# Places in on-chip memory: W_out tiles on one place modulo 256 bytes, token sums in steps of 128 bytes

## The chip, the cores and the metric

One core of a Trainium2 chip runs the program. The metric is device time in microseconds (us): the median of three runs, and beside it one profiled execution, whose trace is what the rows below are read from. TensorE multiplies matrices; for each product it loads a stationary operand (a weight load, PEld in the profile) and then streams a moving operand through it (PE). Both come from the on-chip memory, in which every tile has a place: an offset in bytes within each of the 128 partitions. Results go to the accumulation banks.

## The reference

The program computes block-causal attention for 8 batches of 8 heads, 576 positions and head size 64, and feeds it to a two-layer network.

```python
scores = scale * np.matmul(q, k.transpose(0, 1, 3, 2))
scores = np.where(mask, scores, -1000000000.0)        # blocks of 64
attn = np.exp(scores - max); attn = attn / (sum + 1e-09)
x = (attn @ v) as 4608 tokens of 512
h = x @ w_in                                          # 512 -> 2048
g = h * (1.0 / (1.0 + np.exp(-h)))
out = g @ w_out                                       # 2048 -> 512
```

All of it is in float32, and the weights arrive as 64-bit words.

## The kernel before

The tokens, W_in and W_out are each split into a high and a low part of a reduced float type, and a product is made of three matmuls: high by high, high by low, low by high. The order of the work on every engine is written out by hand, in a long list of steps (`a.load`, `ffn`, `i34.lo:3`, ...); the list is not part of the change, and every engine has the same instructions in the same order before and after it.

**First layer** (`ffn1`, L1063). W_in lies in `wi[0]` (high) and `wi[1]` (low), four rows `c` of 128 inputs each; it is the stationary operand, in pieces of 128 columns. The tokens lie in `xbuf` and are the moving operand, 448, 512 or 256 columns a matmul. Three matmuls follow each other on one row `c`, then three on the next. In the profile they are `h<-x,wi`: the moving tile is named first, the stationary one second. The attention's own matmuls (L719, L824) come between the calls of `ffn1` until about 556 us; the last calls of `ffn1` follow each other without them until about 623 us.

**Second layer** (`Item.prod`, L1140). It multiplies 2x2 blocks by Strassen's scheme in seven products. `Item` n (72 of them, four to a block of 256 tokens) forms seven sums of token quarters ("token sums"), high and low, in one of five slots, `slots()[n % 5]`; they are the stationary operand, 128 columns at a time. `Turned` d (0 to 7) holds the seven sums of W_out's quarters, high and low; it is the moving operand, 256 columns. An item has 42 matmuls: for each of the seven products two halves (d even, d odd), and for each of these the three matmuls high-high, high-low, low-high. Items n with n % 4 = 0 multiply by d = 0 and 1, then 2 and 3, 4 and 5, 6 and 7. In the profile these are `S<-ta,x`, `c<-tb,gc` and so on (S and c are accumulation banks).

Each tile's place modulo 256 bytes, as the program is built before the change:

| tile | role | place modulo 256 |
|---|---|---|
| `wi`, rows c = 0, 1, 2, 3 (8320 bytes each) | W_in, stationary in layer 1 | 128, 0, 128, 0 |
| `x` | tokens, moving in layer 1 | 192 |
| `ta` (d = 0, 1, 2) | W_out, moving in layer 2 | 128 |
| `tb` (d = 3, 4, 5) | W_out, moving | 0 |
| columns of `wi` (d = 6, 7) | W_out, moving | 128 for the first four products, 0 for the last three |
| `gc` (slot 0) | token sums, stationary | 64 for all |
| `x` (slots 1 and 4) | token sums | 192 for all |
| columns of `wi` (slots 2 and 3), 64 bytes on | token sums | 192 and 64 by row, high and low alike |

In slots 2 and 3 the place goes 192, 64, 192, 64, 192 in the course of an item's 42 matmuls, changing after 6, 12, 24 and 36 of them. The function that gives a tile its seven groups is `at`, and `of_wi` and `of_x` give them for columns of `wi` and for halves of `xbuf`.

Of the kernel before, what the change touches and what calls it, by code (L numbers as in the profile page):

```python
# [9 lines left out]
F32 = mybir.dt.float32  # L10
F32R = mybir.dt.float32r
# [8 lines left out]
DM, DFF = 512, 2048  # L20
P = 128
# [10 lines left out]
CT = DM // P  # L32
# [7 lines left out]
SHIFT = 16  # L40
# [357 lines left out]
def fills():  # L398

    out = [((0,), d, None) for d in range(LAG)]  # L400
    out += [((0, 1), d, f) for d in range(LAG, NSTEP) for f in range(2)]
    out += [((1,), d, None) for d in range(LAG)]
    out += [((2, 3), d, f) for d in range(NSTEP) for f in range(2)]
    out += [(("b", b), d, f) for b in range(B) for d in range(NSTEP) for f in range(2)]
    return out
# [39 lines left out]
def attn_ffn(ctx: ExitStack, tc: tile.TileContext, qk, v, qk0, v0, qk1, v1, w_in, w_out, out):  # L445
    nc = tc.nc
    pool = lambda name, bufs=1, **kw: ctx.enter_context(tc.tile_pool(name=name, bufs=bufs, **kw))
    cp = pool("const")
# [14 lines left out]
    pU = pool("pU", space=PSUM)  # L463
    pH = pool("pH", bufs=2, space=PSUM)

    wi = [cp.tile([P, CT, DFF + 2 * SHIFT], F32R, name=f"wi{t}") for t in range(2)]
    cp.tile([P, SHIFT], F32, name="gap0")
    xbuf = cp.tile([P, NX, 2, TB], F32R, name="x")
    cp.tile([P, SHIFT], F32, name="gap1")
    steps = fills()  # L470
    g_dram = {z[:2]: dp.tile([P, 2, width(z[0])], F32, name=f"gd{'_'.join(map(str, z[0]))}_{z[1]}") for z in steps}
    x_full, filled = {}, set()
# [106 lines left out]
    def groups(seven):  # L579

        return [seven[:, 0:2], seven[:, 2:3], seven[:, 3:5], seven[:, 5:7]]
# [2 lines left out]

        return g[0][:, j] if j < 2 else g[1][:, 0] if j == 2 else g[2][:, j - 3] if j < 5 else g[3][:, j - 5]

    def at(t, n):

        return [groups(t[:, 1792 * i + n : 1792 * i + n + 1792].rearrange("p (j m) -> p j m", j=7)) for i in range(2)]

    def of_wi(d, e, n):

        a, b = (slice(256 * k + n, 256 * k + n + 256) for k in (d, e))
        return [[w[:, 0:2, a], w[:, 2:3, a], w[:, 0:2, b], w[:, 2:4, b]] for w in wi]

    def of_x(t):

        def some(n, k):
            s = t[n : n + k]
            step = s[1] - s[0] if k > 1 else 1  # L600
            return slice(s[0], s[-1] + 1, step)

        return [[xbuf[:, some(n, k), i] for n, k in ((0, 2), (2, 1), (3, 2), (5, 2))] for i in range(2)]

    class Turned:

# [9 lines left out]
        def place(u):  # L616
            if u.d < NTA:
                t = pools["ta"].tile([P, 2 * 7 * 256 + (24 if u.d == NTA - 1 else 0)], F32R, tag=f"ta{u.d}", name="ta")
                u.g = at(t, 0)
            elif u.d < 6:  # L620
                t = sp.tile([P, 2, 7, 256], F32R, tag=f"tb{u.d}", name="tb")
                u.g = [groups(t[:, i]) for i in range(2)]
            else:
                u.g = of_wi(2 * u.d - 12, 2 * u.d - 11, 0)

# [450 lines left out]
    class Item:  # L1076
# [44 lines left out]
        def hi(u, k):  # L1121
            if k == 0:
                u.g = slots()[u.n % NSLOT]
            nc.scalar.copy(u.goal(0, k), u.source(k))  # L1124
# [21 lines left out]
    spare = []  # L1146

    def slots():
        if not spare:
            t = sp.tile([P, 2 * 7 * 256 + SHIFT], F32R, tag="gc", name="gc")  # L1150
            spare.extend([at(t, SHIFT), of_x(range(7)), of_wi(4, 5, SHIFT), of_wi(6, 7, SHIFT), of_x(range(8, 15))])
        return spare

    class Out:
# [53 lines left out]
    a, b = First(0), First(1)  # L1208
# [24 lines left out]
    for token in ORDER.split():  # L1233
        name, _, method = token.partition(".")
        if name.startswith("warm:"):
            warm(int(name[5:]))
        elif method:
            method, _, k = method.partition(":")
# [47 lines left out]
```

## Time and profile before

| | |
|---|---|
| median of three runs | 985.79 us (984.91 to 987.05) |
| the profiled execution | 985.77 us |
| its span, first to last instruction | 984.1 us |
| matmuls of layer 1 (L1063) | 1968 |
| matmuls of layer 2 (L1140) | 3024 |

Of the profiled execution, 1.7 us lie outside the span. Matmuls are pipelined: the profile gives each a duration of about 0.28 us for 256 columns, while the next one starts after 0.11 to 0.12 us. So a busy share does not tell how fast TensorE goes; the time from one start to the next does. From a row of the timeline that merges n matmuls, this step is (the row's us minus one duration) / (n - 1), or the difference of two rows' starts divided by the matmuls between them.

### The profile page before, as it was taken

The page shows a single profiled execution, that of the slowest core. Times are in us where ns is not written, and L with a number is a line of the kernel's source. Part 1 is how long each engine was busy: PE and PEld are TensorE (multiplying, and loading weights), DVE is VectorE, ACT ScalarE, POOL GpSimd, SP SyncE. Part 2 cuts the span into 40 slices and gives each one's busy share as a digit, 9 for nine tenths or more (in the row PEclk, how much of TensorE's full clock was granted, in tenths as well). Part 3 has the DMA queues.
Part 4 walks back from the last instruction along what each step waited for, and adds up shares of the span by engine and source line. Part 5 has one row for each costly group of instructions (what it writes and reads, how often), then busy time and mean ns, then how long its engine had stood idle before and what let it go on. Part 6 is the DMA issues. An engine that isn't in the chain of part 4 may idle for free.

```text
span 984.1 us, 20775 instructions
## 1 busy us (share of the span) xinstructions
PE 971.9 (99%) x6922; PEld 878.7 (89%) x6922; DVE 770.3 (78%) x1975; ACT 689.1 (70%) x1557; POOL 618.9 (63%) x724
## 2 busy tenths in 40 slices
PE   7999999999999999999999999999999999999998
PEld 7778778888888888888888899999999999999998
DVE  6868899899899999889999544598677777677661
ACT  5977777777777777777777455997667666767750
POOL 5666977988788787777887556654444443444430
PEclk9999999999999999999999999999999999999999
DMA  9966545554555545555554266655544544454511
GB/s 352 384 196 188 167 140 150 157 152 148 164 149 148 168 141 150 162 144 157 155 153 136 88 207 201 199 172 149 134 131 124 149 133 128 139 141 132 140 52 44
DMA packets 109803, 155.50 MB, mean 158 GB/s; under 512 B 18560, under 2 KB 83072, under 8 KB 109696
## 3 DMA queue, kind: packets, MB, share of 16 engines
q1 hardware_dynamic: 109696, 154.18, 52.4%
q8 instruction: 54, 0.88, 0.4%
q14 instruction: 53, 0.43, 0.1%
HBM read 106.95 MB, written 47.19 MB: 157 GB/s over the span
## 4 chain that ended last, share of the span: by engine, by line
PE 95%; DMA 2%; SPq 1%; DVE 1%; ACT 0%; POOL 0%; issue 0%; DVEq 0%; POOLq 0%
PE h L1063 42%; PE S L1140 24%; PE c L1140 10%; PE S L719 9%; PE U L824 9%; DMA wst<-in_moe_w_in_dram 1%; PE S L1004 1%; DMA raw<-gdb 1%; SPq L1088 1%; PE S L1035 0%; PE S L881 0%; DVE g L1175 0%; SPq L905 0%; POOL x L1128 0%; PE S L966 0%
## 5 line engine op out<-in xcount | busy, mean ns | idle before, releaser
L1063 PE MATMUL h<-x,wi 128*128 128x448 f32 (+2 forms) x1968 | 420.6, 369 | 1.7 <-POOL wi L576 0.9
L1063 PEld LDWEIGHTS h<-x,wi 128*128 128x128 f32 x1968 | 356.8, 188 | 38.3 <-POOL wi L576 1.1
L773 ACT ACTIVATE p<-T 128x512 f32<-128x512 f32 (+1 forms) x192 | 115.7, 614 | 29.3 <-DVE T L762 23.9
L658 DVE TRANSPOSE_TENSOR_REDUCE Mx<-S 64x4 f32<-64x128 f32 (+4 forms) x384 | 130.5, 399 | 6.1 <-PE S L719 5.1
L1069 ACT COPY g<-h 128x448 f32<-128x448 f32 (+1 forms) x160 | 86.1, 538 | 35.0 <-PE h L1063 25.4
L1128 POOL TENSOR_TENSOR x<-raw,x 128x512 fp32r<-128x512 f32 (+1 forms) x58 | 59.4, 1028 | 76.6 <-ACT x L1124 68.1
L779 POOL TENSOR_TENSOR pa<-p 128x448 f32<-128x448 f32 x64 | 73.6, 1151 | 49.7 <-ACT p L773 44.9
L1128 POOL TENSOR_TENSOR wi<-raw,wi 128x512 fp32r<-128x512 f32 (+1 forms) x56 | 57.2, 1025 | 72.2 <-ACT wi L1124 65.0
L700 POOL TENSOR_TENSOR qh<-qk,qh 64x576 fp32r<-64x576 f32 x64 | 91.7, 1433 | 5.3 <-DMA gd<-g 0.4
L719 PE MATMUL S<-qh 128*128 128x448 f32 (+3 forms) x320 | 92.1, 301 | 0.0
L824 PE MATMUL U<-p,v 128*64 128x448 f32 (+3 forms) x640 | 86.5, 416 | 0.0
L719 PE MATMUL S<-ql,qh 128*128 128x448 f32 (+3 forms) x320 | 83.9, 307 | 0.0
L694 ACT CAST qh<-qk 128x1024 fp32r<-128x1024 f32 x64 | 67.0, 1047 | 21.5 <-POOL pa L782 6.8
L704 POOL TENSOR_TENSOR ql<-qk,qh 128x448 fp32r<-128x448 f32 x64 | 73.6, 1151 | 10.6 <-issue 5.9
L824 PEld LDWEIGHTS U<-p,v 128*64 128x64 f32 x640 | 43.2, 136 | 40.8 <-issue 30.0
L1091 ACT ACTIVATE raw<-raw 128x1024 f32<-128x1024 f32 x72 | 76.5, 1063 | 0.0
L765 DVE TENSOR_TENSOR T<-S,MR 128x128 f32<-128x128 f32 (+2 forms) x192 | 73.5, 410 | 0.0
L719 PEld LDWEIGHTS S<-ql,qh 128*128 128x128 f32 (+1 forms) x320 | 57.1, 178 | 6.4
L719 PEld LDWEIGHTS S<-qh 128*128 128x128 f32 (+1 forms) x320 | 56.9, 178 | 3.1 <-issue 0.3
L782 POOL TENSOR_TENSOR pa<-pa,p 128x320 f32<-128x320 f32 x64 | 56.0, 875 | 3.7
L744 ACT COPY m<-m 32x14 f32<-32x14 f32 x192 | 38.8, 202 | 26.2 <-DVE m L740 24.7
L1128 POOL TENSOR_TENSOR gc<-raw,gc 128x512 fp32r<-128x512 f32 (+1 forms) x30 | 30.4, 1019 | 40.7 <-ACT gc L1124 33.2
(198 smaller groups left out, 2082.8 us busy)
## 6 DMA issues: line engine op xcount, KB each, us to landing
qk<-in_qk_dram SPq DMA_DIRECT2D x128, 256.0 KB, 3.9
gdb<-g SPq DMA_DIRECT2D x128, 224.0 KB, 2.6
raw<-gdb SPq DMA_DIRECT2D x64, 256.0 KB, 3.2
v<-in_v_dram SPq DMA_DIRECT2D x64, 160.0 KB, 2.3
wst<-in_moe_w_in_dram SPq DMA_DIRECT2D x16, 512.0 KB, 8.5
wst<-in_moe_w_out_dram SPq DMA_DIRECT2D x16, 512.0 KB, 4.8
gd<-g SPq DMA_DIRECT2D x32, 256.0 KB, 2.8
raw<-gd SPq DMA_DIRECT2D x32, 256.0 KB, 3.5
```

Source lines behind the costliest of these rows:

```text
L658: nc.vector.tensor_reduce(out=out, in_=in_, axis=AX.X, op=op, apply_transpose=True)
L700: nc.gpsimd.tensor_tensor(out=u.qh[r, c], in0=u.raw[r, c], in1=u.qh[r, c], op=ALU.subtract)
L704: nc.gpsimd.tensor_tensor(out=u.ql, in0=u.raw[:, :NQ], in1=u.qh[:, :NQ], op=ALU.subtract)
L719: nc.tensor.matmul(u.ps(c, w, m), u.kk[r, j * P : j * P + m], q[r, q0 : q0 + w], start=qq == 0 and not (ROWS and seg == 2), stop=qq == 1 a ...
L773: nc.scalar.activation(u.p[:, c:e], u.T[:, c:e], AF.Exp, scale=SCALE)
L779: nc.gpsimd.tensor_tensor(out=u.pa, in0=u.p[:, :NQ], in1=u.p[:, 960 : 960 + NQ], op=ALU.add)
L824: nc.tensor.matmul(U[64 * e : 64 * e + 64, q0 : q0 + w], y.vv[:, e, j], z.p[:, c : c + w], start=n == 0, stop=n == 4)
L1063: nc.tensor.matmul(o, wi[wt][:, c, w], x_of(g, c, xt), start=c + k == 0, stop=c == CT - 1 and k == 2)
L1069: nc.scalar.copy(g, hs.pop(z)[:, :n])
L1091: nc.scalar.activation(u.raw, u.raw, AF.Silu)
L1128: e.tensor_tensor(out=u.goal(1, k), in0=u.source(k), in1=u.goal(0, k), op=ALU.subtract)
L1140: nc.tensor.matmul(o, quarter(u.g[a], j)[:, P * e : P * e + P], quarter(turned[d].g[b], TORDER[FACTOR[pr]]), start=u.q == 0 and i % 2 == 0 ...
```

## The change

Rows of `wi` become 8448 bytes (33 times 256), the gap behind `x` grows from 64 to 192 bytes, `tb` gets the same layout as `ta`, and the token sums in `x` and `gc` are laid out with steps of 128 bytes between them.

```diff
-    wi = [cp.tile([P, CT, DFF + 2 * SHIFT], F32R, name=f"wi{t}") for t in range(2)]
+    wi = [cp.tile([P, CT, DFF + 4 * SHIFT], F32R, name=f"wi{t}") for t in range(2)]
     cp.tile([P, SHIFT], F32, name="gap0")
     xbuf = cp.tile([P, NX, 2, TB], F32R, name="x")
-    cp.tile([P, SHIFT], F32, name="gap1")
+    cp.tile([P, 3 * SHIFT], F32, name="gap1")
...
-    def at(t, n):
-
-        return [groups(t[:, 1792 * i + n : 1792 * i + n + 1792].rearrange("p (j m) -> p j m", j=7)) for i in range(2)]
-
-    def of_wi(d, e, n):
-
-        a, b = (slice(256 * k + n, 256 * k + n + 256) for k in (d, e))
+    def at(t, n, pitch=256, step=0):
+
+        out = [[], []]
+        for i, g in enumerate(out):
+            for j, w in ((0, 2), (2, 1), (3, 2), (5, 2)):
+                first = n + (7 * pitch + step) * i + pitch * j + step * (j > 2)
+                g.append(t[:, first : first + pitch * w].rearrange("p (j m) -> p j m", j=w)[..., :256])
+        return out
+
+    def of_wi(d, e, n, step=0):
+
+        a, b = (slice(256 * k + m, 256 * k + m + 256) for k, m in ((d, n), (e, n + step)))
         return [[w[:, 0:2, a], w[:, 2:3, a], w[:, 0:2, b], w[:, 2:4, b]] for w in wi]
 
-    def of_x(t):
-
-        def some(n, k):
-            s = t[n : n + k]
-            step = s[1] - s[0] if k > 1 else 1
-            return slice(s[0], s[-1] + 1, step)
-
-        return [[xbuf[:, some(n, k), i] for n, k in ((0, 2), (2, 1), (3, 2), (5, 2))] for i in range(2)]
+    def of_x(h):
+
+        return at(xbuf[:, 8 * h : 8 * h + 8].rearrange("p n i t -> p (n i t)"), 0, 256 + 2 * SHIFT)
...
-                t = sp.tile([P, 2, 7, 256], F32R, tag=f"tb{u.d}", name="tb")
-                u.g = [groups(t[:, i]) for i in range(2)]
+                t = sp.tile([P, 2 * 7 * 256], F32R, tag=f"tb{u.d}", name="tb")
+                u.g = at(t, 0)
...
-            t = sp.tile([P, 2 * 7 * 256 + SHIFT], F32R, tag="gc", name="gc")
-            spare.extend([at(t, SHIFT), of_x(range(7)), of_wi(4, 5, SHIFT), of_wi(6, 7, SHIFT), of_x(range(8, 15))])
+            t = sp.tile([P, 2 * 7 * 256 + 5 * SHIFT], F32R, tag="gc", name="gc")
+            spare.extend([at(t, SHIFT, 256, 2 * SHIFT), of_x(0), of_wi(4, 5, SHIFT, 2 * SHIFT), of_wi(6, 7, 3 * SHIFT), of_x(1)])
```

`SHIFT` is 16 elements, 64 bytes. The places modulo 256 bytes that come of it:

| tile | before | after |
|---|---|---|
| `wi`, rows 0 to 3 (W_in; stationary in layer 1) | 128, 0, 128, 0 | 128 for all |
| `x` (tokens; moving in layer 1) | 192 | 192 |
| `ta` (W_out) | 128 | 128 |
| `tb` (W_out) | 0 | 128 |
| W_out in `wi` (d = 6, 7) | 128, then 0 | 128 |
| slot 0 (`gc`) | 64 | sums 0 to 2: high 192, low 64; sums 3 to 6: high 64, low 192 |
| slots 1 and 4 (`x`) | 192 | even sums: high 192, low 64; odd sums: high 64, low 192 |
| slot 2 (`wi`) | 192 and 64 by row | sums 0 to 2: 192; sums 3 to 6: 64; high and low alike |
| slot 3 (`wi`) | 192 and 64 by row | 64 for all |

The tiles of the attention all move by the same 1152 bytes, so that their places relative to one another stay.

## Rows read from the trace of the kernel before

**Rows 1.** The page: busy us by engine (share of the span), instructions.
```profile
PE 971.9 (99%) x6922; PEld 878.7 (89%) x6922; DVE 770.3 (78%) x1975; ACT 689.1 (70%) x1557; POOL 618.9 (63%) x724
```

**Rows 2.** The page: the chain that ended last, by engine and by line.
```profile
PE 95%; DMA 2%; SPq 1%; DVE 1%; ACT 0%; POOL 0%; issue 0%; DVEq 0%; POOLq 0%
PE h L1063 42%; PE S L1140 24%; PE c L1140 10%; PE S L719 9%; PE U L824 9%; DMA wst<-in_moe_w_in_dram 1%; PE S L1004 1%; DMA raw<-gdb 1%; SPq L1088 1%; PE S L1035 0%; PE S L881 0%; DVE g L1175 0%; SPq L905 0%; POOL x L1128 0%; PE S L966 0%
```

**Rows 3.** Windows by stage: length, busy us by engine (instructions), granted clock, DMA share, GB/s.
```profile
200.00:400.00 200.00, 200.00 (x1153) 170.01 (x1152) 183.78 (x548) 148.78 (x379) 160.74 (x207) 1.00 0.53 153
...
622.50:984.10 361.60, 356.01 (x3034) 355.23 (x3032) 256.66 (x557) 243.09 (x448) 145.52 (x144) 1.00 0.45 129
```

**Rows 4.** Windows, line L1140 alone: busy us of PE and PEld (instructions), clock, DMA.
```profile
622.50:984.10 361.60, 354.36 (x3024) 353.87 (x3024) 1.00 0.45 129
```

**Rows 5.** Timeline, PE: item 24 (`ta` with `x`), item 15 (`gc`). Start, us, count.
```profile
743.57 2.99 PE L1140 MATMUL S<-ta,x 128*128 128x256 f32 x24
746.39 1.58 PE L1140 MATMUL c<-ta,x 128*128 128x256 f32 x12
...
699.31 2.99 PE L1140 MATMUL S<-wi,gc 128*128 128x256 f32 x24
702.13 1.57 PE L1140 MATMUL c<-wi,gc 128*128 128x256 f32 x12
```

**Rows 6.** Timeline, PE: item 12, `ta` with token sums in `wi` (slot 2).
```profile
684.66 2.89 PE L1140 MATMUL S<-ta,wi 128*128 128x256 f32 x24
687.38 1.52 PE L1140 MATMUL c<-ta,wi 128*128 128x256 f32 x12
```

**Rows 7.** Timeline, PE: item 28, `ta` with slot 3; first ten matmuls, later ones.
```profile
763.30 1.34 PE L1140 MATMUL S<-ta,wi 128*128 128x256 f32 x10
...
764.59 1.64 PE L1140 MATMUL S<-ta,wi 128*128 128x256 f32 x13
766.07 1.52 PE L1140 MATMUL c<-ta,wi 128*128 128x256 f32 x12
```

**Rows 8.** Timeline, PE: item 11, W_out in `wi` with `x`; from its sixth matmul.
```profile
680.38 2.20 PE L1140 MATMUL S<-wi,x 128*128 128x256 f32 x18
682.54 1.57 PE L1140 MATMUL c<-wi,x 128*128 128x256 f32 x12
```

**Rows 9.** Timeline, PE: item 9, threes of `ta` and `tb` with `x`.
```profile
671.35 0.51 PE L1140 MATMUL S<-ta,x 128*128 128x256 f32 x3
671.69 0.52 PE L1140 MATMUL S<-tb,x 128*128 128x256 f32 x3
672.04 0.51 PE L1140 MATMUL S<-ta,x 128*128 128x256 f32 x3
672.39 0.52 PE L1140 MATMUL S<-tb,x 128*128 128x256 f32 x3
672.75 0.51 PE L1140 MATMUL c<-ta,x 128*128 128x256 f32 x3
```

**Rows 10.** Groups of L1063 by shape: form, count, busy us, mean ns, idle before.
```profile
L1063 PE MATMUL h<-x,wi 128*128 128x448 f32 x1536 | 323.8, 367 | 0.0
L1063 PE MATMUL h<-x,wi 128*128 128x512 f32 x336 | 84.2, 401 | 0.0
```

**Rows 11.** Timeline, PE: stretches of layer 1 (256, 512 and 448 columns).
```profile
20.96 2.10 PE L1063 MATMUL h<-x,wi 128*128 128x256 f32 x17
...
41.81 5.04 PE L1063 MATMUL h<-x,wi 128*128 128x512 f32 x21
...
557.33 64.92 PE L1063 MATMUL h<-x,wi 128*128 128x448 f32 x322
```

**Rows 12.** Timeline, PE: layer 1 just after a late weight load.
```profile
435.02 1.80 PE L1063 MATMUL h<-x,wi 128*128 128x448 f32 x8
```

**Rows 13.** Waits, 622 to 985 us: who waited for whom, us, times, longest.
```profile
PEld S L1140 <- DVE g L1175: 1.8, 2, 1.4
...
PE S L1140 <- DVE g L1175: 1.4, 2, 1.1
```

## The prediction

> **What bounds the kernel now.** First the busy shares: PE has work in 99% of the span, no other engine more than 78% [rows 1]. Then the chain that ended last: 95% of it is PE, 42% in the first layer's matmuls and 34% in the second layer's [rows 2]. Then the stages: PE is busy throughout in a stretch of layer 1, and in 356.01 of 361.60 us of layer 2, where VectorE has work in 257 us and ScalarE in 243 [rows 3]. The granted clock is 1.00 in both, the 2.4 GHz level, so what follows isn't the clock. PE waits for another engine only four times in layer 2, 3.2 us together, each time for a VectorE sum [rows 13]. So the time is the number of matmuls times the step from one start to the next, and the change, which leaves every instruction in its order, can only act through that step.
>
> The step isn't the same everywhere, though the matmuls are. In layer 2 all 3024 have 256 columns and an equal weight load; their mean step is 354.36 / 3024 = 117.2 ns [rows 4]. The timeline shows two values instead of a spread. Item 24 (`ta` at place 128, all sums at 192) and item 15 (sums all at 64) go at (2.99 - 0.28) / 23 = 117.8 ns [rows 5]. Item 12, the same `ta` with sums in slot 2, whose place alternates between 192 and 64, goes from 684.66 to 687.38 in 24 steps: 113.3 ns [rows 6]. I call these the slow and the fast step.
>
> **What turns one into the other.** Three rows tell, with the table of places beside them.
> - Item 28 (slot 3, alternating) begins slow, (1.34 - 0.28) / 9 = 117.8, and from its 12th matmul, where the sums go from 64 back to 192, runs at (1.64 - 0.28) / 12 = 113.3 to the end of the row and on [rows 7]. Two more changes of the sums' place (after the 24th and the 36th) don't end it. In item 12 none of four does.
> - Item 11 is fast at (2.20 - 0.28) / 17 = 112.9 ns while the W_out tile lies at 128, and slow at (1.57 - 0.28) / 11 = 117.3 from the product whose W_out lies at 0, with the sums at 192 all along [rows 8]. A change of the moving operand's place ends the fast step.
> - Item 9 changes the moving place every third matmul (`ta` 128, `tb` 0) and goes at (672.75 - 671.35) / 12 = 116.7 ns, between the two [rows 9].
>
> So in these rows: the fast step, once reached, survives any change of the stationary place and any stretch without one; it is lost when the moving place changes; the slow step is left at a change of the stationary place, not at each one, and items with no change at all stay slow for all their 42 matmuls.
>
> **The change, part by part.**
>
> *W_out on one place* (`tb` from 0 to 128, rows of `wi` on one place). It takes away what ends the fast step: the change between `ta` and `tb` inside items n % 4 = 1, the change after the fourth product in items n % 4 = 3, and the one from item to item.
>
> *Token sums in steps of 128 bytes* (`x` and `gc`: slots 0, 1 and 4, three items of five). High and low sums now lie at 192 and 64 in turn, so every group of three matmuls has a change of the stationary place, where before there was none. That is what ends the slow step. Slot 2 keeps two such changes; slot 3 loses its own, but has only to keep what the items before it reached.
>
> Together: if all 3024 went at 113.3 ns, layer 2 would take 342.6 us of PE instead of 354.36, 11.7 less. About 1 us of that is an estimate of what isn't step: the stage's first and last matmul and the four waits each end in a whole matmul of 0.28 us and a late weight load. Of the 10.7 left I take nine tenths, for stretches that fall back after a wait or need some items to turn: **9.6 us**. The bounds: 10.7 if everything turns, and a loss of 3024 x (117.8 - 117.2) = 1.8 us if the parts that are fast now become slow.
>
> *Rows of W_in*. Layer 1 also has its stationary places changed: 128, 0, 128, 0 before, changing every third matmul, and 128 always after. Its moving operand stays at 192. The steps now: 448 columns (64.92 - 0.36) / 321 = 201.1 ns, 512 columns (5.04 - 0.40) / 20 = 232.0, and 256 columns (2.10 - 0.28) / 16 = 113.8 [rows 11]. No row shows layer 1 without the alternation, so this is bounded. Upwards: after one late weight load at 435 us eight matmuls go at (1.80 - 0.37) / 7 = 204.3 ns [rows 12], 3.2 more; over 1536 matmuls [rows 10] that is 4.9 us, and the same on the 336 of 512 columns 1.1: 6.0 us lost. Downwards: the fast step per column, 113.3 / 256 = 0.4427 ns, gives 198.3 for 448 columns and 226.7 for 512, an estimate of a matmul that nothing disturbs: 2.8 x 1536 + 5.3 x 336 = 6.1 us won. Layer 1 is neither at the one nor at the other, and nothing says to which side the loss of alternation moves it: the alternating rows of layer 2 are faster than the constant ones, which speaks for a loss; but the fast step there held through 12 matmuls of one place. I take **0**, the middle, and keep both ends.
>
> *The rest costs nothing I can see.* The same elements are written by the same instructions, in strides instead of runs, on ScalarE, VectorE and GpSimd, none over 71% of layer 2 [rows 3]; were they 3% slower, they would stay hidden. The attention's tiles move as one block, so its matmuls keep their relative places. If PE takes 3% less per item, the VectorE sums that four times came late could come late more often: 3.2 us for four waits [rows 13] makes 0.8 for one more, which the tenth left out covers.
>
> Sum, against the profiled execution's own 985.77 us (the median of the three runs is 985.79): 985.77 - 9.6 - 0 = **976.2 us**.
>
> **A rule against it.** The steps above differ by 4.5 ns with nothing but places to tell them apart [rows 5, 6]. The Trainium skill, "TensorE: Matmul & The Clock Gate", section "Step-by-step: what each phase is for", says that PE has two independent read ports, and that loading the next weights takes no read bandwidth from the running matmul. By that rule places could not matter and the change would give 985.8; the traces don't bear it out, since equal matmuls at equal clock have two steps, and the rival below that goes that way has a small chance.
>
> **The rivals.**
> - *Places are not the cause* (the rule's case): the two steps come with the items' neighbours or their writers, and stay. For it: the slow step isn't left at each change of place. Against it: item 11 turns slow in the middle, at the very product where only the W_out place changes [rows 8]. It gives 985.8 within 1.5. Chance 0.06.
> - *Half locked*: changing the stationary place every second or third matmul is a new rhythm that no row shows; like the moving one in item 9 [rows 9] it could hold the matmuls at a step between, say 115.5 ns. Then 3024 x 1.7 = 5 us are won: 980.7. Chance 0.10.
> - *W_in loses its alternation*: layer 2 turns fast, layer 1 goes to its slow step in most calls, 2 to 6 us: 978 to 982. Chance 0.15.
> - *W_in wins too*: without a change of place layer 1 comes near the undisturbed step, 2 to 6 us: 970 to 974. Chance 0.12.
> - *Slower*: the slow step is what a call begins with, and a stationary on one place keeps it. All of layer 1 now has one place, and pays its whole 6.0 us; slots 2 and 3 lose changes as well. The point from which this decides: if layer 2 gains less than 6.0 us, that is if fewer than six in ten of its matmuls turn fast, the kernel is slower; with none turning it is 985.8 + 6.0 + 1.8 = 993.6, with four in ten 987.5. Against it: a fast step was never lost in a slot by a change of the sums' place. Chance 0.09.
>
> **How the numbers follow.** The forecast (layer 2 fast, layer 1 within 2 us of now) has 0.48: its own range is 974 to 978.5. To hold eight in ten, the range leaves out most of the slower case and the deeper half of the case where W_in wins too: 972 to 987. Faster by over 0.2% (2 us, about what a measurement of this kernel can tell from no change) is the forecast, both W_in cases and the half-locked one, 0.85, less 0.02 for weak ends of these: 0.83. Within 0.2%: 0.07. Slower: 0.10.
>
> **What the changed profile would show.** Layer 2: the busy time of L1140 near 344 us, and timeline rows of 24 matmuls with 2.89 us where they have 2.99, in all slots, those of `tb` and `gc` too; the merged threes of item 9 each 0.34 after the one before. Layer 1: the row of over 300 matmuls near 600 us at 201 ns if I am right to put it at 0, at 204 if the alternation was needed, at 198 if it was a burden. The waits on VectorE sums still some four. The prediction is wrong if timeline rows in `x` or `gc` keep 117.8 although their places alternate, or if layer 1's step moves by more than 1.5 ns.

## The result, and the profile after

The changed kernel takes 974.92 us (median of 4 runs, 974.18 to 975.76), the kernel before in the same comparison 986.42 (984.91 to 987.15): a ratio of 0.9886 [0.9868, 0.9903], 11.5 us faster. The profiled execution takes 975.19 us with a span of 973.2, against 985.77 and 984.1: 10.9 us of span to be found.

The page of the changed kernel, busy us by engine and the chain that ended last by engine, answers to [rows 1, 2]:

```profile
PE 961.0 (99%) x6922; PEld 869.3 (89%) x6922; DVE 768.6 (79%) x1975; ACT 688.4 (71%) x1557; POOL 617.7 (63%) x724
...
PE 89%; DVE 3%; ACT 3%; DMA 2%; issue 1%; SPq 1%; POOL 0%; DVEq 0%; ACTq 0%; POOLq 0%
```

PE has lost 10.9 us of busy time (971.9 to 961.0) with the same 6922 matmuls, its weight loads (PEld) 9.4, and no other engine over 1.7. PE is still the bound, but the chain now passes through VectorE and ScalarE for 6% of the span where it was 1%.

Where the time came from is told by the two layers. The windows of line L1140 alone (length, busy us of PE and PEld with instructions, clock, DMA share, GB/s) answer to [rows 4]:

```profile
620.00:973.20 353.20, 345.06 (x3024) 344.18 (x3024) 1.00 0.47 133
```

Layer 2 has 345.06 us of PE instead of 354.36, 9.3 less, at the same clock. The timeline (start us, us, engine, line, operation, names, tile, count) shows the step. Here are, in order of time, layer 1 with 256, 512 and 448 columns, which answer to [rows 11]; the first matmuls of layer 2; item 8 (slot 3) behind a wait; item 9, the threes of [rows 9]; item 15, the slot `gc` of [rows 5]; item 16, the slot `x`; item 32 (slot 2) with a wait in it:

```profile
19.89 3.10 PE L1063 MATMUL h<-x,wi 128*128 128x256 f32 x24
...
41.57 4.75 PE L1063 MATMUL h<-x,wi 128*128 128x512 f32 x20
...
556.72 64.36 PE L1063 MATMUL h<-x,wi 128*128 128x448 f32 x321
...
620.92 1.57 PE L1140 MATMUL S<-ta,gc 128*128 128x256 f32 x12
...
664.38 1.69 PE L1140 MATMUL S<-ta,wi 128*128 128x256 f32 x12 [1.45 <-DVE g L1175]
665.90 1.57 PE L1140 MATMUL c<-ta,wi 128*128 128x256 f32 x12
...
668.36 0.50 PE L1140 MATMUL S<-tb,x 128*128 128x256 f32 x3
668.70 0.50 PE L1140 MATMUL S<-ta,x 128*128 128x256 f32 x3
669.04 0.50 PE L1140 MATMUL S<-tb,x 128*128 128x256 f32 x3
...
696.58 2.88 PE L1140 MATMUL S<-wi,gc 128*128 128x256 f32 x24
699.30 1.52 PE L1140 MATMUL c<-wi,gc 128*128 128x256 f32 x12
...
701.34 2.88 PE L1140 MATMUL S<-ta,x 128*128 128x256 f32 x24
704.06 1.52 PE L1140 MATMUL c<-ta,x 128*128 128x256 f32 x12
...
777.50 1.52 PE L1140 MATMUL S<-ta,wi 128*128 128x256 f32 x12
779.36 1.68 PE L1140 MATMUL S<-ta,wi 128*128 128x256 f32 x12 [0.33 <-DVE g L1175]
780.88 1.57 PE L1140 MATMUL c<-ta,wi 128*128 128x256 f32 x12
```

The items in `x` and `gc`, slow before, go at (2.88 - 0.28) / 23 = 113.0 and (699.30 - 696.58) / 24 = 113.3 ns; the threes of item 9 follow each other by 0.34. What is left of the slow step stands behind a wait: in item 32 twelve matmuls are fast, PE waits, and the next twelve go at (1.57 - 0.28) / 11 = 117.3. Layer 1 goes at (64.36 - 0.36) / 320 = 200.0 ns instead of 201.1 with 448 columns and at (4.75 - 0.40) / 19 = 228.9 instead of 232.0 with 512. Its last stretch ends earlier: layer 2 begins at 620.92, and before the change, where its first row is this, at 623.10:

```profile
623.10 1.58 PE L1140 MATMUL S<-ta,gc 128*128 128x256 f32 x12
```

PE's waits in layer 2 (waiting engine, line and releaser: us in total, times, longest) answer to [rows 13]:

```profile
PEld S L1140 <- DVE g L1175: 2.5, 3, 1.7
...
PE S L1140 <- DVE g L1175: 1.8, 2, 1.4
...
PE S L1140 <- DVE x L1128: 0.2, 1, 0.2
```

So 10.9 us of span are 2.2 that are won ahead of layer 2 (623.10 - 620.92) and 8.7 of layer 2: 9.3 less busy time, less 0.6 that PE waits longer (2.0 us against 1.4).

### The profile page after: what moved, and what is told of

It reads as the page before. It is cut to its first block, busy times and chain, and to the rows that moved or that the text cites. A ratio compares the mean times of both kernels' runs of the same rounds, so it can differ in the third digit from the quotient of the medians.

```text
span 973.2 us, 20775 instructions
## 1 busy us (share of the span) xinstructions
PE 961.0 (99%) x6922; PEld 869.3 (89%) x6922; DVE 768.6 (79%) x1975; ACT 688.4 (71%) x1557; POOL 617.7 (63%) x724
## 4 chain that ended last, share of the span: by engine, by line
PE 89%; DVE 3%; ACT 3%; DMA 2%; issue 1%; SPq 1%; POOL 0%; DVEq 0%; ACTq 0%; POOLq 0%
PE h L1063 41%; PE S L1140 21%; PE S L719 9%; PE U L824 9%; PE c L1140 8%; DMA wst<-in_moe_w_in_dram 1%; DVE h L1111 1%; DMA raw<-gdb 1%; PE S L1004 1%; ACT raw L1091 1%; SPq L1088 1%; DVE wi L1128 0%; PE S L1035 0%; DVE g L1175 0%; ACT gc L1124 0%
## 5 line engine op out<-in xcount | busy, mean ns | idle before, releaser
L1063 PE MATMUL h<-x,wi 128*128 128x448 f32 (+2 forms) x1968 | 418.4, 368 | 1.7 <-POOL wi L576 0.9
L1063 PEld LDWEIGHTS h<-x,wi 128*128 128x128 f32 x1968 | 356.8, 188 | 36.1 <-POOL wi L576 1.1
```

Source lines behind the costliest of these rows:

```text
L1063: nc.tensor.matmul(o, wi[wt][:, c, w], x_of(g, c, xt), start=c + k == 0, stop=c == CT - 1 and k == 2)
```

## Experiments

**The theories.** Theory one is the prediction's: in layer 2 the step has two values, the fast one is lost when W_out's place changes, and the slow one is left at a change of the sums' place. The rival: it is enough that W_out stays on one place, and the sums' layout does nothing. For layer 1 it had to be found out what the 2.2 us come from. All edits are to the changed kernel; all ratios are to the kernel before.

For some kernels I give each matmul of an item as one letter, worked out from the starts in the trace: F where the next starts within 115 ns, s where it takes 117 to 130, m between, ! where it takes longer (PE paused). A line begins with the number of the item.

**a_sums_still.** W_out stays at 128, all token sums go to 192, so that no place changes anywhere in layer 2.

```diff
-        return at(xbuf[:, 8 * h : 8 * h + 8].rearrange("p n i t -> p (n i t)"), 0, 256 + 2 * SHIFT)
+        x = xbuf[:, 8 * h : 8 * h + 7]
+        return [[x[:, 0:2, i], x[:, 2:3, i], x[:, 3:5, i], x[:, 5:7, i]] for i in range(2)]
...
-            spare.extend([at(t, SHIFT, 256, 2 * SHIFT), of_x(0), of_wi(4, 5, SHIFT, 2 * SHIFT), of_wi(6, 7, 3 * SHIFT), of_x(1)])
+            spare.extend([at(t, SHIFT), of_x(0), of_wi(4, 5, SHIFT), of_wi(6, 7, SHIFT), of_x(1)])
```

> W_out on one place (128) as in the change, but no steps between the token sums: in all five slots every sum, high and low, lies at 192. Nothing in layer 2 changes its place at all. My theory (the slow step of 117.8 ns is left only at a change of the stationary place): it stays slow except where a wait happens to restart it, mean step 117 to 117.8 ns, busy time of layer 2's matmuls near 355 us, and the whole near 985 us, layer 1 being as in the change. Rival one (W_out on one place is what does it): mean step near 113.6 ns as in the change, 975 us. Rival two (the rule that places don't matter): the same as the change, 975 us.

Measured: 982.56 us, median of 10 runs that lie between 974.32 and 985.47; ratio 0.9941 [0.9913, 0.9969]. No other kernel here is spread like this (the next, d_rows_8320, by 5.7 us); the spans themselves go from 972.4 to 983.8 us. The profiled one has a span of 979.5, and its timeline shows what is drawn by lot (the end of item 31 and the first two products of item 32; a wait; the rest; a threes stretch of item 41):

```profile
774.80 1.52 PE L1141 MATMUL c<-wi,x 128*128 128x256 f32 x12
776.16 0.84 PE L1141 MATMUL S<-wi,x 128*128 128x256 f32 x6
776.84 1.52 PE L1141 MATMUL S<-ta,wi 128*128 128x256 f32 x12
778.70 1.68 PE L1141 MATMUL S<-ta,wi 128*128 128x256 f32 x12 [0.33 <-DVE g L1176]
780.22 1.58 PE L1141 MATMUL c<-ta,wi 128*128 128x256 f32 x12
...
821.91 0.52 PE L1141 MATMUL S<-ta,x 128*128 128x256 f32 x3
822.26 0.52 PE L1141 MATMUL S<-tb,x 128*128 128x256 f32 x3
```

The items by letters:

```
 4  FFFFFFFFFFF!!Fssssssssssssssssssssssssssss
 5  ssssssssssssssssssssssssssssssssssssssssss   (6 and 7 alike)
 8  sssssssssss!!ssmFFFFFFFFFFFFFFFFFFFFFFFFFF
 9  FFFFFFFFFFFFFFFFFFFFFFFFFFFFFFFFFFFFFFFFFF   (10 to 31 alike)
32  FFFFFFFFFFF!!Fssssssssssssssssssssssssssss
33  ssssssssssssssssssssssssssssssssssssssssss   (34 to 71 alike)
```

Some 1000 matmuls run fast and some 1670 slow, one after the other, with nothing between them but a pause of 0.33 us. Both steps keep themselves; without a change of place only a pause moves the kernel from the one to the other, in either direction (item 8: slow to fast). The 985 us that were expected are the slow end of the spread: what the expectation put down as the exception, a pause that restarts the step, decides over hundreds of matmuls. The rivals, which have 975 us, fall as rules for the whole: W_out on one place doesn't make the kernel fast, it only stops making it slow.

**c_one_change.** As before, but slot 0 (`gc`) lies at 64 as a whole: the sums' place changes at the borders of every fifth item and nowhere else.

```diff
-            spare.extend([at(t, SHIFT, 256, 2 * SHIFT), of_x(0), of_wi(4, 5, SHIFT, 2 * SHIFT), of_wi(6, 7, 3 * SHIFT), of_x(1)])
+            spare.extend([at(t, 3 * SHIFT), of_x(0), of_wi(4, 5, SHIFT), of_wi(6, 7, SHIFT), of_x(1)])
```

(`of_x` as in a_sums_still.)

> As the run with all sums at 192, but slot 0 has all its sums at 64: the stationary place changes only between items, twice in 210 matmuls. My theory says that the step is a state which keeps itself: slow at first, turned fast at one of the first few returns from 64 to 192, then fast through hundreds of matmuls without any change, until a wait for another engine restarts it. Mean step 113.5 to 116 ns, 975 to 983 us. Rival (each group of three needs its own change, the step follows the places of the last few matmuls only): 117.5 ns, 985 us.

Measured: 974.92 us (974.1 to 978.36, 4 runs), ratio 0.9887 [0.986, 0.9914]: the same as the change. But the profiled run doesn't show that a border healed anything: item 0 is slow, and so is the start of item 1 behind its border (threes 0.35 apart), which turns fast at a pause; each later pause was followed by two to ten slow matmuls and healed inside its own item, before a border came. The time is that of the change; whether the borders earn it, or four good draws, this run leaves open.

**b_tb_at_0.** `tb` goes back to 0, all else stays as in the change.

```diff
-    cp.tile([P, 3 * SHIFT], F32, name="gap1")
+    cp.tile([P, SHIFT], F32, name="gap1")
...
-            t = sp.tile([P, 2 * 7 * 256 + 5 * SHIFT], F32R, tag="gc", name="gc")
-            spare.extend([at(t, SHIFT, 256, 2 * SHIFT), of_x(0), of_wi(4, 5, SHIFT, 2 * SHIFT), of_wi(6, 7, 3 * SHIFT), of_x(1)])
+            t = sp.tile([P, 2 * 7 * 256 + 7 * SHIFT], F32R, tag="gc", name="gc")
+            spare.extend([at(t, 3 * SHIFT, 256, 2 * SHIFT), of_x(0), of_wi(4, 5, SHIFT, 2 * SHIFT), of_wi(6, 7, 3 * SHIFT), of_x(1)])
```

> The change with one part undone: tb (W_out, d = 3 to 5) at place 0, everything else as in the change, token sums in steps included. My theory (a change of the moving place ends the fast step): the 18 items that take ta and tb in turns, 756 matmuls, go at 115.5 to 117.5 ns, the other 54 items stay near 113.6 but for a few matmuls after each such item: 977 to 979 us. Rival (the steps of the token sums alone do it): all near 113.6 ns, 975 us.

Measured: 979.37 us (979.13 to 979.8, 4 runs), ratio 0.9925 [0.9901, 0.9948], 4.5 us slower than the change. The windows of L1140, and the timeline of item 22, whose W_out is `tb` throughout, and of the threes of item 41:

```profile
615.00:985.00 370.00, 349.00 (x3024) 348.46 (x3024) 1.00 0.45 130
```

```profile
731.44 2.93 PE L1140 MATMUL S<-tb,wi 128*128 128x256 f32 x24
734.21 1.52 PE L1140 MATMUL c<-tb,wi 128*128 128x256 f32 x12
...
824.09 0.51 PE L1140 MATMUL S<-tb,x 128*128 128x256 f32 x3
824.44 0.52 PE L1140 MATMUL S<-ta,x 128*128 128x256 f32 x3
824.79 0.52 PE L1140 MATMUL S<-tb,x 128*128 128x256 f32 x3
```

L1140 has 3.9 us more than in the change, and the threes are 0.35 apart. (Layer 2 also begins 1.1 us later, at 621.99, with the same steps in layer 1; that part isn't explained.) Item 22 goes at (2.93 - 0.28) / 23 = 115.2 ns at first and at (1.52 - 0.28) / 11 = 112.7 after. By letters:

```
21 slot 1  FFFsFssmFssmsFsFFFsFsFFFssssFsFFFsFsFFFsFs   ta and tb in turn
22 slot 2  sssssssssssmFFFFFFFFFFFFFFFFFFFFFFFFFFFFFF   tb; sums change after 12
23 slot 3  ssssssssssssssssssssssssssssssssssssssssss   W_out in wi; sums never change
24 slot 4  sssFFFFFFFFFFFFFFFFFFFFFFFFFFFFFFFFFFFFFFF   ta; sums alternate every three
```

This is the cleanest picture of theory one, without a pause in it. W_out moves all through item 21, whose end is slow. Item 22 stays on `tb` and goes on slow until its sums change place, after the 12th matmul. W_out moves once more at the start of item 23: slow again, and slot 3, whose sums never change, stays so for all 42. Item 24 keeps W_out where it is and alternates its sums: three matmuls, then fast. The time comes out above the expected 977 to 979 us; in layer 2 slots 2 and 3 pay too, and not only the items that mix `ta` and `tb`.

**d_rows_8320.** Rows of W_in back to 8320 bytes.

```diff
-    wi = [cp.tile([P, CT, DFF + 4 * SHIFT], F32R, name=f"wi{t}") for t in range(2)]
+    wi = [cp.tile([P, CT, DFF + 2 * SHIFT], F32R, name=f"wi{t}") for t in range(2)]
...
-            spare.extend([at(t, SHIFT, 256, 2 * SHIFT), of_x(0), of_wi(4, 5, SHIFT, 2 * SHIFT), of_wi(6, 7, 3 * SHIFT), of_x(1)])
+            spare.extend([at(t, SHIFT, 256, 2 * SHIFT), of_x(0), of_wi(4, 5, SHIFT, 2 * SHIFT), of_wi(6, 7, SHIFT), of_x(1)])
```

> The change with the rows of W_in back at 8320 bytes: in layer 1 the stationary place alternates between 128 and 0 again; in layer 2 the W_out tiles d = 6, 7 lie at 128 for four products and at 0 for three, and slots 2 and 3 change place by row. Layer 1 should go back to 201.2 ns for 448 columns and 232 for 512 if the rows are what made it quicker (200.1 and 229.6 in the change), 2.6 us in all; if the quicker layer 1 came from somewhere else (places of other tiles), it stays at 200.1. In layer 2 the 18 items with d = 6, 7 lose part of their fast step at the fifth product (some 300 matmuls by 3 ns, 1 us). So 978 to 979 us by my theory, 975 to 976 by the rival.

Measured: 984.94 us (983.48 to 989.15, 10 runs), ratio 0.9987 [0.9973, 1.0002]. My layout was at fault: slots 2 and 3 shared 32 columns, so that the sums of one item overwrote some of the other's, and items waited for one another. PE's waits on the writers of `wi`, which the change doesn't have, come to 2.5 us, and after most of these pauses the step is slow. So the time says nothing on the rows. Layer 1, which the overlap doesn't touch, has steps of 201.3 and 232.5 ns; the next run asks again.

**e_rows_again.** The same row length, with slots 2 and 3 apart, as the kernel before has them.

```diff
-    wi = [cp.tile([P, CT, DFF + 4 * SHIFT], F32R, name=f"wi{t}") for t in range(2)]
+    wi = [cp.tile([P, CT, DFF + 2 * SHIFT], F32R, name=f"wi{t}") for t in range(2)]
...
-            spare.extend([at(t, SHIFT, 256, 2 * SHIFT), of_x(0), of_wi(4, 5, SHIFT, 2 * SHIFT), of_wi(6, 7, 3 * SHIFT), of_x(1)])
+            spare.extend([at(t, SHIFT, 256, 2 * SHIFT), of_x(0), of_wi(4, 5, SHIFT), of_wi(6, 7, SHIFT), of_x(1)])
```

> Again the change with the rows of W_in at 8320 bytes, this time with slots 2 and 3 laid as before the change, so that no two slots share columns (in the run d_rows_8320 they shared 32 columns, which made items wait for one another). Layer 1: 201.3 ns for 448 columns and 232.4 for 512, as before the change, against 200.1 and 229.6 in it: 2.5 us more if the rows are the cause. Layer 2: the fast step is lost in the 18 items with d = 6, 7 at their fifth product, where W_out goes from 128 to 0, and found again in the next items with steps in their sums: mean near 114.3 ns, 2 to 3 us more. Together 979 to 980.5 us. If layer 1 owed its gain to something else: 977.5.

Measured: 979.18 us (978.65 to 979.89, 4 runs), ratio 0.9932 [0.9917, 0.9947], 4.3 us slower than the change. Timeline: a stretch of layer 1, then item 51 (W_out in `wi`, at 128 for its first four products and at 0 for the rest; sums in `x`), then item 55, the same with sums in `gc`:

```profile
559.67 58.49 PE L1063 MATMUL h<-x,wi 128*128 128x448 f32 x290
...
872.96 2.88 PE L1140 MATMUL S<-wi,x 128*128 128x256 f32 x24
875.68 1.59 PE L1140 MATMUL c<-wi,x 128*128 128x256 f32 x12
877.11 0.87 PE L1140 MATMUL S<-wi,x 128*128 128x256 f32 x6
...
892.15 2.88 PE L1140 MATMUL S<-wi,gc 128*128 128x256 f32 x24
894.87 1.54 PE L1140 MATMUL c<-wi,gc 128*128 128x256 f32 x12
```

Layer 1 is back at (58.49 - 0.36) / 289 = 201.1 ns, the step before the change, so its gain comes from the rows. And item 51 falls slow at the 25th matmul, where W_out goes to 0. But it stays slow for the 18 left, (1.59 - 0.28) / 11 = 119.1 ns, although its sums alternate every three; seven items in slots 1 and 4 do so, while in slot 0 (item 55, (1.54 - 0.28) / 11 = 114.5 ns) they recover after three. So a change of the sums' place isn't always enough: it depends on where W_out lies as well. In the change W_out lies at 128 throughout.

The traces tell which change it is. I count, in all of them but d_rows_8320, the places where PE was slow and only the sums moved, with no pause. Where the sums moved from 64 bytes short of W_out's place to 64 bytes past it (to 192 with W_out at 128, to 64 with W_out at 0), the step turned fast in 47 of 59 cases; where they moved the other way, in none of 44. A three whose places alternate takes the high sum twice and then the low one: with the high sum past W_out's place 49 of 64 slow threes were fast right after, with the high sum short of it 14 of 72. In the items above, from the product where W_out goes to 0, slot 0 has its high sums at 64 (the last product aside) and slots 1 and 4 have them at 192. To lie past W_out's place isn't enough without the change: in a_sums_still all sums do.

**f, g, h, i, j: the place of the tokens.** These move `x`, and nothing else of layer 1, to 128, 0, 64, 160 and 224 modulo 256; its operands then differ by 0, 128, 192, 32 and 96 bytes, where the change has 64 (`x` at 192, `wi` at 128). The gaps around `x` and the first argument of `at` move so that layer 2 keeps its places: gap 0 of 0, 32, 48, 8 and 24 elements, gap 1 of 64, 32, 16, 56 and 40, and an offset of 16, 48, 32, 8 and 56. The edit of g:

```diff
-    cp.tile([P, SHIFT], F32, name="gap0")
+    cp.tile([P, 2 * SHIFT], F32, name="gap0")
...
-    cp.tile([P, 3 * SHIFT], F32, name="gap1")
+    cp.tile([P, 2 * SHIFT], F32, name="gap1")
...
-        return at(xbuf[:, 8 * h : 8 * h + 8].rearrange("p n i t -> p (n i t)"), 0, 256 + 2 * SHIFT)
+        return at(xbuf[:, 8 * h : 8 * h + 8].rearrange("p n i t -> p (n i t)"), 3 * SHIFT, 256 + 2 * SHIFT)
```

> The change with x moved to place 128, where the rows of W_in lie too (difference 0 in layer 1); token sums at 192 and 64 as in the change, so layer 2 stays near 113.5 ns. Theory one, that layer 1 settles in a steady pattern set by the difference of places: another step than 200.1 ns, between the undisturbed 198.3 and 206; at difference 0 both operands start on the same place, so I expect it slower, 202 to 206 ns, 977 to 984 us. Theory two, that only changes of place count and not the place: 200.1 ns and 975 us.

> The change with x at place 0, W_in at 128 (difference 128 in layer 1), layer 2 as in the change. Theory one (the difference sets the step): as far apart as two places modulo 256 can be, so the quickest of the four: 198 to 199.5 ns for 448 columns, 972 to 974 us. Theory two (only changes count): 200.1 ns, 975 us.

> The change with x at place 64, W_in at 128 (difference 192 in layer 1 where the change has 64), layer 2 as in the change. Layer 2 showed the same two steps at differences of 64 and 192. So by both theories layer 1 stays at 200.1 ns and the whole at 975 us; if the order of the two places counts (which operand is ahead), it moves by more than 1 ns a step, 1.5 us or more in all.

> The change with x at place 160, so 32 bytes after W_in's 128 where the change has 64 (steps so far for 448 columns by difference: 0: 203.3, 64: 200.1, 128: 203.7, 192: 202.1 ns). Layer 2 as in the change, 113.5 ns. If the step in layer 1 goes smoothly with the difference, it lies between those of 0 and 64: 200.5 to 203 ns, 976 to 979 us. If 32 bytes are enough to keep weight loads and the moving stream apart, 198.3 to 200 ns and a version quicker than the change, 972 to 975 us.

> The change with x at place 224, 96 bytes after W_in. Layer 2 as in the change. Smooth theory: between the steps of 64 and 128, 200.5 to 203.5 ns for 448 columns, 976 to 980 us. If the best place lies past 64: 198.3 to 200 ns, 972 to 975 us.

Measured, with the mean step of layer 1 over all its uninterrupted pairs of starts (1425 pairs with 448 columns, 289 or 290 with 512), and of layer 2:

| kernel | `x` - `wi`, modulo 256 | us | ratio | 448 columns, ns | 512, ns | layer 2, ns |
|---|---|---|---|---|---|---|
| f_x_at_128 | 0 | 979.76 | 0.9939 [0.9924, 0.9954] | 203.3 | 229.2 | 113.5 |
| i_x_at_160 | 32 | 979.36 | 0.9928 [0.9908, 0.9948] | 202.8 | 233.0 | 113.5 |
| the change | 64 | 974.92 | 0.9886 [0.9868, 0.9903] | 200.2 | 229.6 | 113.6 |
| j_x_at_224 | 96 | 982.85 | 0.9967 [0.9955, 0.9979] | 205.3 | 233.2 | 113.5 |
| g_x_at_0 | 128 | 981.65 | 0.9955 [0.994, 0.997] | 203.7 | 232.4 | 113.5 |
| h_x_at_64 | 192 | 978.33 | 0.9921 [0.9904, 0.9937] | 202.1 | 233.2 | 113.5 |
| e_rows_again | 64 and 192 in turn | 979.18 | 0.9932 [0.9917, 0.9947] | 201.3 | 232.4 | 114.1 |
| before | 64 and 192 in turn | 986.42 | 1 | 201.3 | 232.2 | 116.9 |

The timeline of j_x_at_224 shows the slowest of these, (56.94 - 0.36) / 275 = 205.7 ns:

```profile
561.40 56.94 PE L1063 MATMUL h<-x,wi 128*128 128x448 f32 x276
```

Layer 2 is unmoved in all five, so their times are layer 1's: for f, 1536 x 3.1 - 336 x 0.4 ns = 4.6 us more than the change, measured 4.8; for i, j, g and h 5.1, 9.0, 6.3 and 4.1 against 4.4, 7.9, 6.7 and 3.4. The mean step of layer 1 is set by the two places, within 5 ns; the expectation that g would be quickest failed, and so did the one that h, with 192 for 64, would change nothing: which of the two lies ahead matters. The step isn't smooth in the difference either: 96 is slower than 64 and 128 on its sides, and both ranges expected of j failed. For 448 columns alternating 64 and 192 gives 201.3, about the mean of the two alone (200.2 and 202.1); for 512 it gives 232.4, nearer to 233.2 than to 229.6. No place tried gives a shorter time than the change's.

## Why the prediction was right

**The mechanism** stands. It was to be seen in [rows 5 to 9] that the step has two values and what moves it between them; a_sums_still and b_tb_at_0 show it with one cause each taken away. The prediction saw that not every change of the sums' place ends the slow step, but not which one does (e_rows_again). The stated signs came: L1140 at 345.06 us (near 344), rows of 24 matmuls with 2.88 in `gc` and `x`, the threes 0.34 apart.

**Layer 2, 9.6 us.** Measured 9.3 of busy time, less 0.6 of longer waits: 8.7. The tenth left out was for "stretches that fall back after a wait or need some items to turn"; the letters show both, in items 0, 1, 4, 8, 32, 52 and 53. Three of them in the change:

```
 8 slot 3  !ssssssssss!!ssssssssssssssssssssssssssssF
32 slot 2  FFFFFFFFFFF!!ssssssssssssssssssssssmFFFFFF
52 slot 2  FFFFFFFFFFFFssmsssssssssssssssssssssssssss
```

Slot 3, which never changes its place, keeps the fall to its end, and item 9 with its alternating sums is fast. Slot 2 changes after the 12th and the 36th matmul, and in item 32 the fall ends at the 36th, in the change and in b, f, g, h, i and j alike. Item 52 falls without a wait just where its sums go from 192 to 64, which seems to go against the prediction's sentence that a fast step was never lost by such a change. But in c_one_change slot 2 has no change there, and its item 52 has two steps of 122 ns at the same matmul: something short disturbs this place whatever the sums do, and in c it is over at once. With item 53 behind it, it costs some 70 x 4.5 ns, 0.3 us. The likely cause is a wait too short to show as one. In items 8, 32 and 52 the 13th matmul waits for a VectorE sum (L1175); here are that sum and the row of the 13th matmul, first of item 32, which pauses, then of item 52:

```profile
778.89 0.41 DVE L1175 TENSOR_TENSOR g<-S,u 128x256 f32<-128x256 f32 x1
779.36 1.68 PE L1140 MATMUL S<-ta,wi 128*128 128x256 f32 x12 [0.33 <-DVE g L1175]
...
874.20 0.41 DVE L1175 TENSOR_TENSOR g<-S,u 128x256 f32<-128x256 f32 x1
874.77 1.58 PE L1140 MATMUL S<-ta,wi 128*128 128x256 f32 x12
```

In item 32 the sum ends 0.06 us before the matmul starts, in item 52 0.16 us. That is so in all eight kernels with the disturbance (0.15 to 0.16); before the change and in e_rows_again, which don't have it, the sum ends 0.19 and 0.24 us before. No run moves this sum alone, so the cause is not shown.

**The waits.** I counted four, 3.2 us. [rows 13] show two pauses, each once for the weight load and once for the matmul behind it. It entered the sum only as cover for late sums, so it moved nothing.

**Layer 1, 0 us.** This is the term that was mis-sized: 2.2 us were won. By the means of the table it is 1536 x 1.1 = 1.7 us with 448 columns and 336 x 2.6 = 0.9 with 512, 2.6 together; the 0.4 between isn't traced, and in a, b and c, with the layer 1 of the change, the start of layer 2 itself differs by 1.5 us (620.49 to 621.99). The bounds of 6 us on both sides held, but neither of their rows spoke of the right thing. The row after a late weight load [rows 12] was taken as what layer 1 costs without its alternation, and the step per column of layer 2 as what it could reach. The runs show that the step depends on where `x` and `wi` lie to each other: the change leaves only the better of two differences, 64, which nothing in the prediction chose, so this gain is luck; with another one it would have lost up to 205.3 - 201.3 = 4.0 ns, 6 us, at the same "loss of alternation". The mark that I set, that the prediction is wrong if the step of layer 1 moves by more than 1.5 ns, held for 448 columns (1.1) and not for 512 (2.6).

**The rest, 0 us**, holds as far as the busy times tell: VectorE, ScalarE and GpSimd each have 0.7 to 1.7 us less than before.

**The rivals.** That places are not the cause, and the half-locked step at 115.5 ns, fell with the rows of items 9, 15 and 16. That the kernel gets slower fell twice over: far more than six in ten matmuls turned fast (of 3013 steps 2848 are within 115 ns, before the change 687 of 3017), and layer 1 lost nothing. That W_in wins too is what happened, at the lower end of its 2 to 6 us; the time, 974.9, lies in the forecast's own 974 to 978.5 because two misses partly cancel: layer 1 gave 2.2 more than the forecast's 0, layer 2 0.9 less. By the rule of the Trainium skill that was weighed ("TensorE: Matmul & The Clock Gate", "Step-by-step: what each phase is for") the time would have stayed at 985.8; the traces don't agree: in b_tb_at_0 the place of `tb` alone takes the busy time of layer 2 from 345.06 to 349.00 us, at a granted clock of 1.00 in both.

## What to carry to other kernels

Read the step from start to start, not the busy share: a PE that is 99% busy had 1.2% to give in places alone. Where equal matmuls have two steps, look up the operands' places modulo 256 bytes, keep the moving one on one place, and give the stationary one changes, so that a pause is healed soon; the change that healed here is the one to 64 bytes past the moving operand's place. A kernel without any change may time well in one run and 11 us worse in the next. (Why modulo 256: 128 bytes of `tb` change the step in b_tb_at_0, while in items 9 to 31 of a_sums_still, all fast, places differ by multiples of 256.) For a long stretch with both operands fixed, try some differences between them: here the best and the worst are 8 us apart, and the order can't be guessed from a few.

## What was not expected of the hardware

- The two steps of layer 2 keep themselves over a thousand matmuls and more, and a pause of 0.33 us can turn either into the other (a_sums_still, items 8 and 32). Ten runs of one and the same program lie between 974.32 and 985.47 us.
- With 448 and 512 columns I followed only the mean; single steps are spread (196 to 211 ns for 448 in the change). The mean for 448 goes from 200.2 to 205.3 ns with the difference of places, and for 448 and 512 columns the order of the differences isn't the same (a difference of 0 is the best for 512, 229.2, and among the slow for 448, 203.3).
- With 256 columns the step of layer 1 has moved as well: of its 91 steps that the trace gives, 45 were within 115 ns before the change, none in it and 64 in h_x_at_64, which has `wi` 64 bytes past `x` where the change has it 64 short. In neither of the two does anything change its place, so here the difference counts. There are too few of these steps to matter.
- Open: what in the chip holds the state, why only the change to 64 bytes past the moving operand's place ends the slow step, why 12 of 59 such changes didn't, and whether the late sum is what disturbs item 52. No run here tells.
